# A recurrent attention layer with a SwiGLU layer behind it: the first feed-forward group in two halves of 256 columns, under a new emission order

## The chip, the cores and the metric

The kernel runs on one core of one Trainium2 chip. The metric is the device time of one execution in microseconds (us), lower is better. One execution was also recorded by the hardware profiler; its record (the trace) lists every instruction with start, duration and what it waited for. Names of engines: PE is the matrix engine, DVE the vector engine, ACT the scalar engine, POOL the fourth compute engine, SP the engine whose queue issues most transfers.

## The reference, cut to what matters

Inputs r, k, v, w have the shape (batch 4, head 8, time 768, 48), u is (8, 48). Per batch and head a 48x48 state is decayed by w and fed by k and v; its read-out by r, over all heads, is one row of 384 numbers per batch and time. These 3072 rows go through a normalised SwiGLU layer with 1536 inner columns.

```
for t in range(S):
    cur = einsum('bhd,bhe->bhde', u[None] * kt, vt)
    y[:, :, t] = einsum('bhd,bhde->bhe', rt, state + cur)
    state = wt[:, :, :, None] * state + einsum('bhd,bhe->bhde', kt, vt)
...
rms = sqrt(mean(x * x, axis=-1) + 1e-06)
xn = x / rms * rms_g
g = xn @ w_gate
out = (g * sigmoid(g) * (xn @ w_val)) @ w_out
```

## The kernel before, in words

Time is cut into six chunks of 128 steps. A chunk n of a batch j is a unit (n, j); there are 24 of them. A unit is handled in matrix form by small functions, each called a step and written as fn.n.j:

- load_r, load_k, load_v, load_w bring 192 KB each through the queue of SP (L259, L271). For chunks 0 and 1 one load_w of 384 KB (L271, form 128x8x96) serves both chunks of a batch. load_gv and load_wo bring the three weight matrices through the queue of POOL (L351, L354); load_gv.0.0 and 0.1 are the first 512 columns of w_gate and w_val, load_gv.1.0 and 1.1 the other 1024.
- ln (ACT), cs_mm (PE, L404 to L422), exp_r and exp_k (ACT), w_tot, r_mul and k_mul make the decayed r and k. k_mul runs on POOL or DVE, by a set of units called K_POOL (L459).
- rk_pe and rk_tr (L482, L489, L491) or a transposing transfer (L487) turn r and k; q_mm (L500, L502) gives the scores, q_mask_e and q_mask_o mask them (DVE L507, L515, or ACT L511 and POOL L518), y_mm (L545, L548) sums, st_mm and st_new carry the state. bonus_mul, bonus_sum, bonus_v are the u term (POOL, DVE, POOL).
- x_add, x_sq, x_rstd, xn_mul, then xn_pe and xn_out (L586, L596) or xn_tr and xn_gain, write the normalised, turned rows of the unit into its columns of a tile xnt.

The feed-forward layer works on groups of 512 columns, four units each. COL gives a unit its group and place: group 0 holds (0,0), (0,1), (1,0), (1,1) in this order, group 1 holds (0,2), (1,2), (0,3), (1,3), and groups 2 to 5 are the chunks 2 to 5. A group has 12 gate_mm and 12 val_mm steps. Each fills one PSUM bank of 512 columns with three matmuls of 512 columns for one of the 12 blocks of inner columns (L617). For a group named in HALF it fills the bank with two blocks of 256 columns, six matmuls in all (L622): steps f = 0 to 5 read only the first 256 columns of the group, f = 6 to 11 only the last 256. silu (ACT, L251) and h_mul (DVE, L643 or L646) take the banks away. o_mm (L660) multiplies with w_out, o_out copies, out_dma stores.

No scheduler orders this. The table ORDER at the head of the file lists all steps; the code runs through it once, and every engine executes its own steps in that order. A number behind a colon, as in `q_mm.1.1:7`, puts that many matmuls on a tile of zeros in front of the step (L238, L240); their result is overwritten. PSUM banks come from three rings (two slots for gate and cs_mm, two for val and cs_mm, four for the rest), and sets such as CAST_ACT, K_POOL, RK_DVE, ODD_DVE, RSTD_ACT and OUT_DVE say which engine does a step of a unit.

```
HALF = (1,)
...
def half_of_group(f):
    h, p = f // (FC // 2), f % (FC // 2)
    return slice(h * TS // 2, (h + 1) * TS // 2), 2 * p
...
for fn, n, j in steps:
    fns[fn](n, j)
```

Of the kernel before, what the change touches and what calls it, by code (L numbers as in the profile page):

```python
# [26 lines left out]
load_k.0.1 load_w.0.3 load_v.0.1 exp_r.0.0 exp_k.0.0 r_mul.0.0 cast_v.0.0 load_r.0.1 bonus_mul.0.0 load_k.1.1
bonus_sum.0.0 bonus_v.0.0 k_mul.0.0 cs_mm.1.0 load_r.1.1 load_v.1.1 load_v.1.0 load_w.0.2 rk_pe.0.0:2 rk_tr.0.0
exp_r.1.0 w_tot.1.0 w_tot.0.0 st_mm.0.0 r_mul.1.0 st_new.0.0 q_mm.0.0:4 load_k.0.3 load_r.0.3 load_r.0.2 load_k.0.2
load_v.0.2 ln.0.1 q_mask_o.0.0 exp_k.1.0 cs_mm.0.1 exp_r.0.1 k_mul.1.0 exp_k.0.1 rk_pe.1.0 load_v.0.3 rk_tr.1.0  # L30
bonus_mul.1.0 q_mask_e.0.0 load_k.1.3 load_r.1.2 load_k.1.2 load_r.1.3 load_v.1.2 bonus_mul.0.1 load_w.2.1 load_w.2.0
load_v.1.3 load_w.2.3 q_mm.1.0:2 cs_mm.1.1 exp_r.1.1 exp_k.1.1 r_mul.0.1 k_mul.0.1 w_tot.0.1 q_mask_o.1.0
bonus_sum.1.0 load_gv.0.1 cast_v.0.1 load_r.2.0 bonus_sum.0.1 r_mul.1.1 load_w.2.2 rk_pe.0.1:2 ln.0.3 y_mm.0.0
rk_tr.0.1 st_mm.0.1:4 x_add.0.0 q_mask_e.1.0 st_new.0.1 cs_mm.0.3:3 bonus_v.0.1 cast_v.1.0 q_mm.0.1:1 y_mm.1.0
k_mul.1.1 bonus_v.1.0 cast_v.1.1 q_copy_o.0.1 x_sq.0.0 bonus_mul.1.1 load_r.2.1 x_add.1.0 exp_r.0.3 load_r.2.2
x_sq.1.0 load_r.2.3 load_k.2.0 q_mask_e.0.1 w_tot.1.1 rk_pe.1.1:1 rk_tr.1.1 q_mm.1.1:7 q_mask_o.1.1 load_gv.0.0
q_mask_o.0.1 y_mm.0.1:8 g_mm.0.0 bonus_sum.1.1 ln.0.2 x_rstd.1.0 xn_mul.1.0 x_rstd.0.0 xn_mul.0.0 exp_k.0.3
bonus_v.1.1 load_gv.1.0 q_mask_e.1.1 x_add.0.1 x_sq.0.1 x_rstd.0.1 y_mm.1.1 x_add.1.1 k_mul.0.3 xn_pe.1.0:2 xn_pe.0.0
cs_mm.0.2 g_out.0.0 xn_out.1.0 x_sq.1.1 xn_mul.0.1 xn_out.0.0 r_mul.0.3 st_mm.1.1:3 x_rstd.1.1 st_mm.1.0 xn_mul.1.1
xn_pe.0.1 xn_out.0.1 w_tot.0.3 rk_pe.0.3:3 xn_pe.1.1 xn_out.1.1 exp_r.0.2 exp_k.0.2 r_mul.0.2 val_mm.0.0:4 gate_mm.0.3  # L40
silu.0.3 val_mm.0.3 rk_tr.0.3 w_tot.0.2 st_new.1.1 load_gv.1.1 k_mul.0.2 bonus_mul.0.2 q_mm.0.3 h_mul.0.3 st_new.1.0
gate_mm.0.2 gate_mm.0.0 rk_pe.0.2 silu.0.0 silu.0.2 val_mm.0.2 q_mask_e.0.3 h_mul.0.0 gate_mm.0.5 gate_mm.0.1 silu.0.5
silu.0.1 val_mm.0.1 rk_tr.0.2 q_copy_o.0.3 h_mul.0.1 bonus_mul.0.3 bonus_sum.0.3 h_mul.0.2 gate_mm.0.6:1
gate_mm.0.11:1 q_mm.0.2 cast_v.0.2 silu.0.6 silu.0.11 q_mask_o.0.2 gate_mm.0.8 val_mm.0.6 q_mask_e.0.2 cast_v.0.3
st_mm.0.2 val_mm.0.11 q_mask_o.0.3 h_mul.0.6 val_mm.0.5 y_mm.0.3 y_mm.0.2 bonus_sum.0.2 bonus_v.0.2 load_wo.0.0
load_wo.1.0 bonus_v.0.3 silu.0.8 h_mul.0.11 cs_mm.1.2 load_wo.2.0 h_mul.0.5 exp_k.1.2 x_add.0.2 st_new.0.2 exp_r.1.2
k_mul.1.2 cs_mm.1.3 exp_k.1.3 st_mm.0.3 exp_r.1.3 val_mm.0.8 val_mm.0.7 w_tot.1.2 r_mul.1.2 x_add.0.3 gate_mm.0.4
w_tot.1.3 r_mul.1.3 rk_pe.1.2 gate_mm.0.7 k_mul.1.3 h_mul.0.8 silu.0.4 x_sq.0.3 bonus_mul.1.2 x_rstd.0.3 rk_tr.1.2
silu.0.7 rk_pe.1.3 gate_mm.0.10 val_mm.0.4 h_mul.0.7 x_sq.0.2 rk_tr.1.3 load_k.2.1 load_k.2.3 load_v.2.1 load_v.2.0
load_k.2.2 q_mm.1.2 val_mm.0.9 cast_v.1.2 xn_mul.0.3 silu.0.10 q_copy_o.1.2 h_mul.0.4 q_mask_o.1.2 gate_mm.0.9  # L50
xn_pe.0.3 val_mm.0.10 st_new.0.3 q_mm.1.3 bonus_sum.1.2 x_rstd.0.2 q_mask_e.1.2 xn_out.0.3 y_mm.1.2 h_mul.0.10
q_mask_e.1.3 silu.0.9 h_mul.0.9 o_mm.0.3 ln.2.1 xn_mul.0.2 bonus_v.1.2 bonus_mul.1.3 q_mask_o.1.3 st_mm.1.2 xn_pe.0.2
cs_mm.2.1 ln.2.0 x_add.1.2 cs_add.2.1 x_sq.1.2 cs_mm.2.0 exp_r.2.1 o_out.0.3 xn_out.0.2 x_rstd.1.2 cast_v.1.3
cs_add.2.0 bonus_sum.1.3 w_tot.2.1 ln.2.3 exp_k.2.1 exp_r.2.0 o_mm.0.0 y_mm.1.3 xn_mul.1.2 o_out.0.0 bonus_v.1.3
r_mul.2.0 x_add.1.3 exp_k.2.0 ln.2.2 x_sq.1.3 o_mm.0.2 o_out.0.2 w_tot.2.0 r_mul.2.1 x_rstd.1.3 st_mm.1.3 cs_mm.2.3
xn_pe.1.2 cs_add.2.3 xn_out.1.2 cs_mm.2.2 exp_r.2.3 cs_add.2.2 load_k.3.3 w_tot.2.3 o_mm.0.1 xn_mul.1.3 r_mul.2.3
st_new.1.2 exp_k.2.2 val_mm.1.1 gate_mm.1.1 exp_r.2.2 exp_k.2.3 w_tot.2.2 val_mm.1.2 xn_pe.1.3 r_mul.2.2 gate_mm.1.2
st_new.1.3 silu.1.1 silu.1.2 k_mul.2.0 bonus_mul.2.0 out_dma.0.0 k_mul.2.1 cast_v.2.1 k_mul.2.3 h_mul.1.1 rk_tr.2.0
rk_tr.2.1 gate_mm.1.3 silu.1.3 bonus_mul.2.2 k_mul.2.2 xn_out.1.3 bonus_sum.2.0 h_mul.1.2 val_mm.1.5 gate_mm.1.4
silu.1.4 val_mm.1.4 rk_tr.2.3 gate_mm.1.8 st_mm.2.1 gate_mm.1.5 silu.1.8 h_mul.1.4 val_mm.1.8 load_v.2.2 silu.1.5  # L60
cast_v.2.0 st_new.2.1 rk_tr.2.2 o_out.0.1 h_mul.1.8 gate_mm.1.9 gate_mm.1.10 val_mm.1.3 load_w.3.3 load_v.2.3
load_r.3.3 load_w.3.1 out_dma.0.3 load_w.3.0 out_dma.0.1 load_r.3.0 bonus_v.2.0 bonus_mul.2.3 bonus_sum.2.2 h_mul.1.5
bonus_mul.2.1 cast_v.2.2 load_k.3.0 load_w.3.2 q_mm.2.0 load_k.3.1 silu.1.9 silu.1.10 q_copy_o.2.1 h_mul.1.3
q_mask_o.2.0 q_mask_e.2.0 q_mask_e.2.1 gate_mm.1.7 gate_mm.1.0 silu.1.0 val_mm.1.0 y_mm.2.0 gate_mm.1.6 val_mm.1.9
bonus_sum.2.3 h_mul.1.0 x_add.2.0 load_r.3.1 x_sq.2.0 silu.1.6 out_dma.0.2 h_mul.1.9 val_mm.1.10 h_mul.1.10 q_mm.2.2
gate_mm.1.11 val_mm.1.6 cast_v.2.3 q_copy_o.2.2 silu.1.7 silu.1.11 ln.3.0 x_rstd.2.0 xn_mul.2.0 q_mask_e.2.3
bonus_sum.2.1 q_mask_e.2.2 q_mask_o.2.1 load_v.3.3 load_w.4.1 load_r.3.2 ln.3.1 bonus_v.2.1 bonus_v.2.2 q_mask_o.2.3
h_mul.1.6 q_mask_o.2.2 bonus_v.2.3 st_mm.2.0 st_new.2.0 o_mm.1.0 y_mm.2.1 load_k.3.2 x_add.2.1 y_mm.2.3 val_mm.1.7
y_mm.2.2 cs_mm.3.0 st_mm.2.3 val_mm.1.11 x_add.2.3 x_sq.2.3 ln.3.3 x_sq.2.1 xn_pe.2.0 cs_mm.3.1 o_out.1.0 o_mm.1.1
out_dma.1.0 h_mul.1.7 cs_add.3.0 exp_k.3.0 x_add.2.2 cs_add.3.1 st_new.2.3 x_rstd.2.3 xn_mul.2.3 ln.3.2 x_sq.2.2  # L70
exp_r.3.0 x_rstd.2.1 k_mul.3.0 x_rstd.2.2 xn_out.2.0 exp_k.3.1 exp_r.3.1 xn_mul.2.1 xn_mul.2.2 h_mul.1.11 o_mm.1.2
r_mul.3.1 w_tot.3.0 k_mul.3.1 w_tot.3.1 xn_pe.2.1 bonus_mul.3.3 r_mul.3.0 o_out.1.2 xn_out.2.1 o_out.1.1 ln.4.1
cs_mm.3.3 xn_pe.2.2 cs_add.3.3 exp_r.3.3 rk_tr.3.1 rk_tr.3.0 cs_mm.3.2 cs_add.3.2 xn_pe.2.3 o_mm.1.3 bonus_mul.3.1
exp_r.3.2 xn_out.2.3 exp_k.3.2 w_tot.3.3 xn_out.2.2 w_tot.3.2 val_mm.2.2 st_mm.2.2 k_mul.3.2 exp_k.3.3 bonus_mul.3.0
r_mul.3.3 r_mul.3.2 gate_mm.2.8 gate_mm.2.2 val_mm.2.10 load_v.3.1 silu.2.8 silu.2.2 o_out.1.3 k_mul.3.3 st_new.2.2
h_mul.2.2 load_v.3.0 load_r.4.1 rk_tr.3.2 gate_mm.2.10 q_mm.3.0 cast_v.3.3 silu.2.10 q_copy_o.3.0 q_mask_e.3.1
bonus_sum.3.0 bonus_v.3.0 q_mask_o.3.0 cast_v.3.0 load_v.4.3 rk_tr.3.3 load_r.4.0 out_dma.1.2 gate_mm.2.9 val_mm.2.11
gate_mm.2.11 silu.2.9 h_mul.2.10 q_mask_e.3.0 val_mm.2.9 gate_mm.2.4 q_copy_o.3.1 bonus_sum.3.3 silu.2.11 bonus_v.3.3
h_mul.2.11 y_mm.3.0 val_mm.2.4 gate_mm.2.7 x_add.3.0 q_mm.3.2 h_mul.2.9 bonus_mul.3.2 silu.2.4 h_mul.2.4 load_v.3.2
gate_mm.2.3 cast_v.3.2 val_mm.2.3 val_mm.2.8 silu.2.3 q_copy_o.3.2 x_sq.3.0 q_copy_o.3.3 silu.2.7 load_k.4.0  # L80
load_k.4.1 load_w.4.0 x_rstd.3.0 xn_mul.3.0 q_mask_e.3.2 bonus_sum.3.1 gate_mm.2.5 h_mul.2.3 bonus_sum.3.2 h_mul.2.8
load_r.4.2 st_mm.3.3 val_mm.2.7 q_mask_e.3.3 st_mm.3.2 gate_mm.2.1 val_mm.2.1 silu.2.5 silu.2.1 q_mask_o.3.2
bonus_v.3.2 gate_mm.2.6 gate_mm.2.0 xn_pe.3.0 y_mm.3.2 st_new.3.2 load_w.5.0 cast_v.3.1 h_mul.2.1 h_mul.2.7 st_new.3.3
bonus_v.3.1 q_mask_o.3.1 out_dma.1.3 y_mm.3.1 val_mm.2.0 load_w.4.2 x_add.3.2 q_mask_o.3.3 silu.2.0 silu.2.6 h_mul.2.0
# [629 lines left out]
```

## Time and profile before

| what | value |
|---|---|
| time, median of 3 runs | 204.41 us (203.04, 204.41, 204.47) |
| span of the profiled execution | 202.2 us, 4604 instructions |
| median time less that span | 2.2 us |
| busy PE, DVE, ACT, POOL | 191.3, 157.5, 135.0, 124.4 us |
| moved by DMA | 32.42 MB, mean 160 GB/s |

The profiled execution's own time is not listed beside its span; the 2.2 us between its span and the median is what lies around a span here. Busy time is the union of an engine's instructions. A row of the timeline gives start, length, engine, line, operation, tiles, shapes and count, and in brackets the idle time before it and what ended it. A row of a windows view gives, for one stretch, busy time and number of instructions of each engine.

### The profile page before, as it was taken

Reading aid. Unit: us, or ns where it says so; the run is one execution under the profiler, and the core shown is the slowest. Engines: PE = TensorE matmul, PEld = TensorE weight load, DVE = VectorE, ACT = ScalarE, POOL = GpSimd, SP = SyncE. Lnnn points to the kernel's source line nnn. Section 1 sums busy time; section 2 is a strip of 40 time slices with the busy share of each in tenths; the row PEclk is TensorE's granted clock in tenths of the full one; section 3 lists DMA queues with packets and bytes.
Section 4 is the critical chain, followed back from the end, with each engine's and each line's share of the span. In section 5 each row is a group of like instructions: output and inputs, shape, how many; then the busy total and the mean of one; then the engine's idle time right before and its main releaser. Section 6 shows DMA issues by size and latency. Waiting matters only on the chain.

```text
span 202.2 us, 4604 instructions
## 1 busy us (share of the span) xinstructions
PE 191.3 (95%) x1677; PEld 121.9 (60%) x1694; DVE 157.5 (78%) x307; ACT 135.0 (67%) x278; POOL 124.4 (62%) x178
## 2 busy tenths in 40 slices
...
GB/s 144 231 234 207 212 208 202 195 179 208 206 184 225 160 212 191 210 185 188 199 176 215 237 188 203 183 190 108 134 179 104 0 23 99 0 117 0 63 115 99
DMA packets 121567, 32.42 MB, mean 160 GB/s; under 512 B 116420, under 2 KB 120392, under 8 KB 121544
## 3 DMA queue, kind: packets, MB, share of 16 engines
...
q10 hardware_dynamic: 8, 0.00, 0.0%
...
## 4 chain that ended last, share of the span: by engine, by line
PE 65%; ACT 3%; DMA 2%; DVE 2%; issue 1%; SPq 0%; DVEq 0%; ACTq 0%
PE ps_av L617 7%; PE ps_bu L617 7%; PE ps_au L617 7%; PE ps_bv L617 6%; PE ps_qx L660 6%; PE ps_qv L660 6%; PE ps_qu L660 5%; PE ps_qz L660 4%; PE ps_au L622 2%; PE ps_bu L622 2%; DMA rkT<-rk 2%; PE ps_av L622 2%; PE ps_bv L622 2%; ACT L249 1%; PE ps_au L419 1%; PE ps_qv L500 1%
## 5 line engine op out<-in xcount | busy, mean ns | idle before, releaser
L660 PEld LDWEIGHTS <-ht 128*128 128x128 bf16 x300 | 28.1, 98 | 17.5 <-DVE ht L646 1.0
L251 ACT ACTIVATE sg<-ps_av 128x512 bf16<-128x512 f32 x36 | 21.5, 597 | 22.8 <-PE ps_av L617 18.0
L646 DVE TENSOR_TENSOR ht<-ps_bv,sg 128x512 bf16<-128x512 f32 x29 | 19.9, 687 | 13.9 <-PE ps_bv L617 12.9
L251 ACT ACTIVATE sg<-ps_au 128x512 bf16<-128x512 f32 x36 | 21.5, 596 | 11.5 <-PE ps_au L617 7.7
L617 PEld LDWEIGHTS <-wg_sb 128*128 128x128 bf16 x180 | 19.2, 114 | 15.9 <-issue 0.6
L617 PEld LDWEIGHTS <-wv_sb 128*128 128x128 bf16 x180 | 19.2, 114 | 15.7 <-issue 0.5
L465 POOL TENSOR_TENSOR ruk<-rt,kt 128x384 f32<-128x384 f32 x24 | 24.0, 1001 | 3.7 <-DMA kt<-in_k_dram 2.8
L475 POOL TENSOR_TENSOR ydiag<-vt,diag 128x384 f32<-128x384 f32 x24 | 20.4, 859 | 9.4 <-DVE diag L470 9.1
L617 PE MATMUL ps_av<-xnt,wg_sb 128*128 128x512 bf16 x88 | 25.0, 381 | 0.3
L466 POOL TENSOR_TENSOR ruk<-ruk,u_bc 128x384 f32<-128x384 f32 x24 | 24.0, 1001 | 1.9
L617 PE MATMUL ps_bu<-xnt,wv_sb 128*128 128x512 bf16 x86 | 24.8, 380 | 0.4
L646 DVE TENSOR_TENSOR ht<-ps_bu,sg 128x512 bf16<-128x512 f32 x31 | 21.3, 686 | 4.8 <-PE ps_bu L617 3.1
L617 PE MATMUL ps_au<-xnt,wg_sb 128*128 128x512 bf16 x87 | 23.6, 380 | 0.1
L617 PE MATMUL ps_bv<-xnt,wv_sb 128*128 128x512 bf16 x82 | 23.2, 380 | 0.2
L459 POOL TENSOR_TENSOR rk<-kt,ek 128x384 bf16<-128x384 f32 x16 | 15.9, 1001 | 9.7 <-ACT ek L251 5.9
L249 ACT ACT_TABLE_LOAD x14 | 18.0, 1283 | 1.9 <-PEq L698 1.6
L660 PE MATMUL ps_qx<-wo_sb,ht 128*128 128x384 bf16 x96 | 17.1, 326 | 0.2 <-DVE ht L646 0.2
L558 ACT ACTIVATE junk<-xb 128x384 bf16<-128x384 f32 x24 | 12.5, 522 | 6.3 <-DVE xb L553 6.2
L571 ACT ACTIVATE xn<-xb,rstd 128x384 bf16<-128x384 f32 x24 | 14.2, 609 | 0.6 <-POOL rstd L567 0.5
L470 DVE TENSOR_REDUCE diag<-ruk 128x8 f32<-128x384 f32 x24 | 13.1, 544 | 1.9 <-POOL ruk L466 1.9
L660 PE MATMUL ps_qv<-wo_sb,ht 128*128 128x384 bf16 (+1 forms) x84 | 13.8, 314 | 0.0
L251 ACT ACTIVATE lw<-wt 128x384 bf16<-128x384 f32 (+1 forms) x20 | 11.6, 583 | 2.8 <-DMA wt<-in_w_dram 2.7
...
## 6 DMA issues: line engine op xcount, KB each, us to landing
...
wg_sb<-in_moe_w_gate_dram POOLq DMA_DIRECT2D x1, 768.0 KB, 9.2
```

What stands on the lines that cost most here:

```text
L249: nc.scalar.preload_act_table_set(table_name)
L251: return nc.scalar.activation(**kw).ins
L459: eng.tensor_tensor(out=rk[:, n % 2, j, 1, :, 0:D], in0=inp["k", n, j], in1=bank["cs_k", n, j][:, 0:DM].rearrange("p (h d) -> p h d", h=H) ...
L465: nc.gpsimd.tensor_tensor(out=ruk[n, j], in0=inp["r", n, j], in1=inp["k", n, j], op=ALU.mult)
L466: nc.gpsimd.tensor_tensor(out=ruk[n, j], in0=ruk[n, j], in1=u_bc, op=ALU.mult)
L470: nc.vector.tensor_reduce(out=diag[n, j].rearrange("p h o -> p (h o)"), in_=ruk[n, j], axis=mybir.AxisListType.X, op=ALU.add)
L475: nc.gpsimd.tensor_tensor(out=ydiag[n, j], in0=inp["v", n, j], in1=diag[n, j].to_broadcast([128, H, D]), op=ALU.mult)
L571: nc.scalar.activation(out=xn, in_=xb[n, j], func=AF.Copy, scale=rstd[n, j][:, 1:2])
L617: nc.tensor.matmul(ps, lhsT=units(ws, c, f), rhs=x[:, c, :], start=(c == 0), stop=(c == KC - 1))
L622: nc.tensor.matmul(ps[:, i * TS // 2:(i + 1) * TS // 2], lhsT=units(ws, c, f + i), rhs=x[:, c, cols], start=(i == 0 and c == 0), stop=(i = ...
L646: nc.vector.tensor_tensor(out=ht[n][:, f, :], in0=v, in1=sg, op=ALU.mult)
L660: nc.tensor.matmul(ps[:, cols], lhsT=ht[n][:, f, b * L:(b + 1) * L], rhs=wo_sb[:, f, cols], start=(f == 0), stop=(f == FC - 1))
```

## The change

HALF becomes (0, 1): group 0 too is computed in halves, the first from chunk 0 of batches 0 and 1, the second from chunk 1 of the same batches. The whole table ORDER is another one, without any number behind a colon, and eight sets are drawn anew. Functions and buffer counts stay as they are; every line number is one lower than before. The lines of the two sets Q_PAIR and OLD_DVE gain only a comma.

```
 ORDER = """
-load_r.0.0 load_w.0.0 u_mm.0.0 ln.0.0 load_v.0.0 load_k.0.0 cs_mm.0.0:2 load_r.1.0 load_w.0.1 u_out.0.0 load_k.1.0
...
+load_w.0.0 load_r.0.0 load_w.0.2 load_k.1.0 ln.0.0 load_v.0.0 cast_v.0.0 load_r.1.0 g_mm.0.0 u_mm.0.0 cs_mm.1.0
...
-    CAST_ACT = sel("00 01 02 03 20 21 30 31 33 40 43 53")
+    CAST_ACT = sel("01 10 12 20 21 23 30 33 50 51 53")
-    K_POOL = sel("02 10 20 21 22 23 30 31 32 33 40 42 43 50 51 53")
+    K_POOL = sel("02 03 12 13 21 22 23 30 31 32 40 41 43 50 52 53")
-    RK_DVE = sel("00 02 03 10 11 12 13")
-    ODD_DVE = sel("00 02 10 11 13 20 23 40 43 52")
-    RSTD_ACT = sel("00 10 11 13 20 32 33")
-    OUT_DVE = sel("00 01 10 13 20 21 22 30 33 40 42 50 52 53")
+    RK_DVE = sel("00 02 03 12 13")
+    ODD_DVE = sel("00 01 02 10 11 13 20 22 32 33 42 43 50")
+    RSTD_ACT = sel("00 01 10 11 23 33 42")
+    OUT_DVE = sel("00 02 11 13 21 22 30 31 32 41 43 51 53")
...
-    HALF = (1,)
+    HALF = (0, 1,)
```

Three places show what the new table does to the engines' own order. First the queue of SP at the start of the program, before; rt, kt, vt and wt are the tiles for r, k, v and w, and the units are, from the top, r(0,0), w of batch 0, v(0,0), k(0,0), r(1,0), w of batch 1, k(1,0) and k(0,1), w of batch 3, v(0,1).

```order
L259 DMA rt<-in_r_dram 128x8x48
L271 DMA wt<-in_w_dram 128x8x96
L259 DMA vt<-in_v_dram 128x8x48
L259 DMA kt<-in_k_dram 128x8x48
L259 DMA rt<-in_r_dram 128x8x48
L271 DMA wt<-in_w_dram 128x8x96
L259 DMA kt<-in_k_dram 128x8x48 x2
L271 DMA wt<-in_w_dram 128x8x96
L259 DMA vt<-in_v_dram 128x8x48
```

The same queue after: w of batch 0, r(0,0), w of batch 2, k(1,0), v(0,0), r(1,0), w of batch 1, k(0,0) and k(0,1).

```order
L270 DMA wt<-in_w_dram 128x8x96
L258 DMA rt<-in_r_dram 128x8x48
L270 DMA wt<-in_w_dram 128x8x96
L258 DMA kt<-in_k_dram 128x8x48
L258 DMA vt<-in_v_dram 128x8x48
L258 DMA rt<-in_r_dram 128x8x48
L270 DMA wt<-in_w_dram 128x8x96
L258 DMA kt<-in_k_dram 128x8x48 x2
```

Counted in loads of 192 KB, k(0,0) moved from the 5th to the 11th place, and v(0,1), a few rows further down, from the 13th to the 22nd. The second place is POOL's order from the first issue of a feed-forward weight to the last, before; ruk is bonus_mul's tile, ydiag bonus_v's, vb the cast v, rstd the scale of x_rstd.

```order
L351 DMA wv_sb_128<-in_moe_w_val_dram 128x3x512
L475 TENSOR_TENSOR ydiag<-vt,diag 128x384
L389 CAST vb<-vt 128x384
L475 TENSOR_TENSOR ydiag<-vt,diag 128x384
L389 CAST vb<-vt 128x384
L465 TENSOR_TENSOR ruk<-rt,kt 128x384
L466 TENSOR_TENSOR ruk<-ruk,u_bc 128x384
L351 DMA wg_sb_126<-in_moe_w_gate_dram 128x3x512
L518 AFFINE_SELECT qts<-qts 128x512
L475 TENSOR_TENSOR ydiag<-vt,diag 128x384
L351 DMA wg_sb_127<-in_moe_w_gate_dram 128x3x1024
```

After, over the same stretch and a little further:

```order
L350 DMA wv_sb_128<-in_moe_w_val_dram 128x3x512
L474 TENSOR_TENSOR ydiag<-vt,diag 128x384
L350 DMA wg_sb_126<-in_moe_w_gate_dram 128x3x512
L474 TENSOR_TENSOR ydiag<-vt,diag 128x384 x2
L388 CAST vb<-vt 128x384
L350 DMA wg_sb_127<-in_moe_w_gate_dram 128x3x1024
L458 TENSOR_TENSOR rk<-kt,ek 128x8x48
L464 TENSOR_TENSOR ruk<-rt,kt 128x384
L465 TENSOR_TENSOR ruk<-ruk,u_bc 128x384
L350 DMA wv_sb_129<-in_moe_w_val_dram 128x3x1024
```

The first three issues stand closer together now, and the last, w_val's other 1024 columns, stands behind k_mul and bonus_mul of unit (0,3); before, only two short operations of x_rstd (L566, L567) stood between the third and the last. The third place is DVE, from the last sum of group 0's units to the tile that the feed-forward matmuls read (xb is x_add's tile, xnt the group's), before:

```order
L507 TENSOR_TENSOR qts<-ps_qz,mask_lt 128x512
L553 TENSOR_TENSOR xb<-ps_qv,ydiag 128x384
L553 TENSOR_TENSOR xb<-ps_qx,ydiag 128x384
L459 TENSOR_TENSOR rk<-kt,ek 128x8x48
L382 COPY gT<-ps_qu 128x3
L596 TENSOR_TENSOR xnt<-ps_qz,gT 128x3x128
L596 TENSOR_TENSOR xnt<-ps_qv,gT 128x3x128
```

After:

```order
L552 TENSOR_TENSOR xb<-ps_qv,ydiag 128x384
L506 TENSOR_TENSOR qts<-ps_qz,mask_lt 128x512
L534 TENSOR_TENSOR st<-ps_qu,wcol 128x384
L514 TENSOR_TENSOR qts<-ps_qx,mask_lt 128x512
L552 TENSOR_TENSOR xb<-ps_qu,ydiag 128x384
L595 TENSOR_TENSOR xnt<-ps_qv,gT 128x3x128
L595 TENSOR_TENSOR xnt<-ps_qx,gT 128x3x128
```

Both masks of unit (1,1) and a state update now stand between the sums of (0,1) and (1,1), and the two xnt writes behind them are those of (0,0) and (0,1), all that the first half of group 0 reads; the writes of (1,0) and (1,1) come later. On PE two gate steps and one val step of the first half stand ahead of the first step of the second half; the xn_pe of (1,0) and (1,1) stand between them.

More of the change, by code (lines that the diff above doesn't have):

```diff
@@ L25 @@
 ORDER = """
-load_r.0.0 load_w.0.0 u_mm.0.0 ln.0.0 load_v.0.0 load_k.0.0 cs_mm.0.0:2 load_r.1.0 load_w.0.1 u_out.0.0 load_k.1.0
[L27 to L84, printed above, removed]
-ln.4.0 cast_v.4.3 val_mm.2.6 h_mul.2.6 y_mm.3.3 cs_mm.4.1 load_r.4.3 load_k.4.3 val_mm.2.5 cs_mm.4.0 x_add.3.1
@@ new lines @@
+xn_pe.0.0 st_mm.1.1 y_mm.1.1 x_sq.0.1 x_sq.1.0 x_rstd.0.1 exp_k.0.3 k_mul.0.3 x_add.1.1 xn_out.0.0 x_rstd.1.0
+xn_mul.0.1 xn_mul.1.0 bonus_mul.0.3 load_gv.1.1 xn_pe.0.1 xn_out.0.1 w_tot.0.2 r_mul.0.2 x_sq.1.1 k_mul.0.2 rk_pe.0.3
+x_rstd.1.1 gate_mm.0.0 xn_pe.1.0 gate_mm.0.1 xn_mul.1.1 st_new.1.1 st_mm.1.0 rk_tr.0.3 xn_out.1.0 load_k.1.2 xn_pe.1.1
+val_mm.0.1 xn_out.1.1 silu.0.0 silu.0.1 q_mm.0.3 gate_mm.0.7 load_w.2.1 val_mm.0.0 gate_mm.0.6 st_new.1.0 h_mul.0.1
+q_mask_e.0.3 h_mul.0.0 silu.0.7 silu.0.6 load_v.1.2 val_mm.0.6 gate_mm.0.8 val_mm.0.7 gate_mm.0.9 bonus_mul.0.2
```

137 lines of the change are left out of this document (95 added, 42 removed).

## The prediction

> **What bounds the kernel now.** I read the page's busy times first, then PE by stretches, then what PE waits for behind the start.
>
> ```profile
> span 202.2 us, 4604 instructions
> PE 191.3 (95%) x1677; PEld 121.9 (60%) x1694; DVE 157.5 (78%) x307; ACT 135.0 (67%) x278; POOL 124.4 (62%) x178
> ```
>
> PE is busy for 95% of the span. The windows view, cut at the first feed-forward matmul (30.21 us) and at PE's end (199.03), says where the rest lies. PE is the first number behind the length of the stretch.
>
> ```profile
> core 0: us, PE busy (x) PEld busy (x) DVE busy (x) ACT busy (x) POOL busy (x), PEclk, DMA share, GB/s
> 0.00:30.21 30.21, 24.25 (x284) 16.16 (x285) 22.14 (x51) 18.06 (x40) 21.78 (x38) 1.00 1.03 206
> 30.21:199.03 168.82, 167.02 (x1394) 105.72 (x1409) 135.04 (x256) 116.91 (x239) 102.63 (x141) 1.00 0.73 153
> 199.03:202.20 3.17, 0.00 (x0) 0.00 (x0) 0.36 (x1) 0.00 (x0) 0.00 (x0) 0.86 0.27 96
> ```
>
> In the middle PE idles 168.82 - 167.02 = 1.8 us. So the time is a start of 30.2 us, a stretch in which PE is the bound, and an end of 3.2 us. Whatever comes off PE's work there comes off the time, and each new wait of PE is added to it. Moving loads and vector work about changes nothing by itself. Of PE's waits from 29 us on the view of waits names two:
>
> ```profile
> PE ps_qu L500 <- DMA rkT<-rk: 0.6, 1, 0.6
> PE ps_qx L660 <- DVE ht L646: 0.2, 1, 0.2
> ```
>
> The start differs in kind: PE's 24.25 us there hold many matmuls on zeros. The L240 group by stretches (the L238 group adds 30 matmuls, all before 30 us):
>
> ```profile
> 12.00:30.00 18.00, 6.30 (x32) 2.85 (x32) 1.00 1.13 211
> 36.00:39.00 3.00, 0.65 (x2) 0.20 (x2) 1.00 1.16 218
> ```
>
> **Part 1: the halves themselves.** A step of group 1, already in halves, and one of group 2 in the chain of work:
>
> ```profile
> 66.53 0.66 PE ps_bv L622 x6
> 92.85 0.65 PE ps_au L617 x3
> ```
>
> Six matmuls of 256 columns take as long as three of 512, within 0.01 us (0.655 against 0.648 by the steps' distances). 24 steps cost 24 x 0.007 = **+0.17 us**. silu and h_mul read banks of the same 512 columns, so ACT and DVE pay nothing. No work is saved: the halves only permit the first half to start before chunk 1 is ready. As the order rows in the sections above show, the table uses that for three steps only.
>
> **Part 2: the zero matmuls go.** Those before 30 us stand in front of steps that wait, so their time is a wait otherwise, and its cover is the chain that the start hangs on (part 3). The two at 36 to 39 us stand between real matmuls:
>
> ```profile
> 36.94 0.33 PE L240 MATMUL ps_av<-zero 128*128 128x384 bf16 x1
> 37.10 0.81 PE L617 MATMUL ps_av<-xnt,wg_sb 128*128 128x512 bf16 x3
> 37.74 0.33 PE L240 MATMUL ps_au<-zero 128*128 128x384 bf16 x1
> 37.91 0.81 PE L617 MATMUL ps_au<-xnt,wg_sb 128*128 128x512 bf16 x3
> ```
>
> From start to next start they take 0.16 and 0.17: **-0.33 us**, all on the path.
>
> **Part 3: the start, with late loads.** Two POOL rows give the pace of the loads: bonus_mul waits for k(0,0), fifth in units of 192 KB; the first cast waits for v(1,0), eighteenth.
>
> ```profile
> 7.08 1.00 POOL L465 TENSOR_TENSOR ruk<-rt,kt 128x384 f32<-128x384 f32 x1 [2.84 <-DMA kt<-in_k_dram]
> 19.11 0.50 POOL L389 CAST vb<-vt 128x384 bf16<-128x384 f32 x1 [0.62 <-DMA vt<-in_v_dram]
> ```
>
> (19.11 - 7.08) / 13 = 0.925 us a load, with the queue full. k(0,0), now eleventh, is there at 7.08 + 6 x 0.925 = 12.6 us. k_mul.0.0 follows, and rk_pe.0.0 starts at 13.1 instead of 9.98. v(0,1), now twenty-second, lands at 19.11 + 4 x 0.925 = 22.8; its cast takes 0.5, so y_mm.0.1 starts at 23.4 at the earliest and, behind DVE's masks, I estimate 24.7. It started at 24.28. The rows from there:
>
> ```profile
> 9.98 0.70 PE L482 MATMUL ps_qv<-ident,rk 128*128 128x128 bf16 x8
> 24.28 0.19 PE L548 MATMUL ps_qv<-vb,qts 128*128 128x48 bf16 x1
> 25.92 0.56 DVE L553 TENSOR_TENSOR xb<-ps_qx,ydiag 128x384 f32<-128x384 f32 x1 [0.30 <-PE ps_qx L548]
> 29.40 0.81 PE L240 MATMUL ps_bv<-zero 128*128 128x384 bf16 x4
> 30.21 0.81 PE L617 MATMUL ps_bv<-xnt,wv_sb 128*128 128x512 bf16 x2
> 32.58 0.84 PE L617 MATMUL ps_au<-xnt,wg_sb 128*128 128x512 bf16 x3
> 16.03 0.36 PE L548 MATMUL ps_qz<-vb,qts 128*128 128x48 bf16 x8
> 18.72 0.55 DVE L535 TENSOR_TENSOR st<-ps_qu,wcol 128x384 bf16<-128x384 f32 x1
> 24.14 0.68 DVE L507 TENSOR_TENSOR qts<-ps_qz,mask_lt 128x512 bf16<-128x512 f32 x1
> 29.93 1.28 ACT L249 ACT_TABLE_LOAD   x1
> ```
>
> Behind y_mm.0.1 DVE has x_add (0.56), a mask (0.68), st_new (0.55), a mask (0.68), then x_add.1.1 (0.56) behind its y_mm (0.36): about 3.4 us, so x_add.1.1 ends near 28.2 instead of 26.48. The xnt writes of (0,0) and (0,1) end a microsecond later, at some 29.6, and the first gate starts there, 0.6 ahead of 30.21. Its bank is free again only after silu, which stands behind xn_mul.1.1 and the table load of 1.28: about 32.8. So the fourth feed-forward step starts at 32.8, where it started at 32.58 before. With the matrix engine at full pace the early half gains nothing: the bounds of this term are -0.6 (the head start is kept) and +0.2.
>
> What the zeros covered is PE's own pace. The same two matmuls of cs_mm, cold and later:
>
> ```profile
> 6.35 0.85 PE L404 MATMUL ps_au<-lw,mw 128*128 128x384 bf16 x2
> 6.99 0.40 PE L408 MATMUL ps_au<-mw,lw 128*128 128x1 bf16 x8
> 11.80 0.50 PE L404 MATMUL ps_au<-lw,mw 128*128 128x384 bf16 x2
> 12.13 0.34 PE L408 MATMUL ps_au<-mw,lw 128*128 128x1 bf16 x8
> ```
>
> From L404 to L408 it is 0.64 us first and 0.33 later: half pace until PE had worked through some 6 us without a pause. (The windows' granted clock says 1.00 all along; it is the distances that show it.) In the changed kernel it waits from about 9 to 13 us, and between 24 and 29.6 its real work is y_mm, st_mm, q_mm, xn_pe and rk_pe: an estimated 2.1 us of 5.6 by their counts and the distances of such rows. If that lets the pace drop, three feed-forward steps (1.95 us), xn_pe, st_mm and q_mm (0.8) run at half pace: +2.7 less the 0.6 of head start, and up to 1 us more where PE is the chain before. I take **+1.9 us**; bounds -0.6 and +3.7. I lean to the slow side since the nearest row is the cold one, in which PE had just been idle.
>
> The Trainium skill, page "TensorE: Matmul & The Clock Gate", Part 1, says that the clock is halved by default, is released after about 3.4 us of sustained work, and is halved again after an idle window of as much. The trace agrees on the factor of two and shows about 6 us instead of 3.4 here. By that rule a wait such as 9 to 13 us could close the gate, but the thinner work from 13 to 29 would leave it open, and this term would be about 0; that outcome is the first rival.
>
> **Part 4: the weights.** The last three issues on POOL's queue, and k_mul of a unit of chunk 0 there:
>
> ```profile
> 23.15 0.81 POOL L351 DMA_DIRECT2D wg_sb<-in_moe_w_gate_dram  x1
> 25.35 0.80 POOL L351 DMA_DIRECT2D wg_sb<-in_moe_w_gate_dram  x1
> 27.36 0.85 POOL L351 DMA_DIRECT2D wv_sb<-in_moe_w_val_dram  x1
> 30.00 0.99 POOL L459 TENSOR_TENSOR rk<-kt,ek 128x384 bf16<-128x384 f32 x1 [1.78 <-ACT ek L251]
> ```
>
> From the view of DMA issues, the KB and the us from issue to landing of the two large parts:
>
> ```profile
> wg_sb<-in_moe_w_gate_dram POOLq DMA_DIRECT2D x1, 768.0 KB, 9.2
> wv_sb<-in_moe_w_val_dram POOLq DMA_DIRECT2D x1, 768.0 KB, 11.5
> ```
>
> The last w_val part was issued at 27.36 and landed at 27.36 + 11.5 = 38.9, the w_gate part before it at 25.35 + 9.2 = 34.5; its first reader came at 39.66. Now it stands behind k_mul.0.3 and bonus_mul.0.3, three operations of 1.0, the first of which waits for exp_k.0.3: some 30.7, so it lands between 39.3 (4.4 behind a w_gate part that itself lands some 0.4 later than now) and 30.7 + 11.5 = 42.2. Its first reader, val_mm.0.8, is the 13th step: 32.8 + 9 x 0.655 + 0.45 = 39.2, or 41 at half pace. The wait is 0 to 3; with the slow start most of it is covered. I take **+0.3**.
>
> **Part 5: the rest of the order.** Sums of work on every engine hardly move: DVE gains three masks of 0.68 and loses two rkT copies and one o_out. PE idles 1.8 us in the middle now. It can lose all of that (-1.8): between the last cs_mm and q_mm.4.0 stand six feed-forward steps behind o_mm.2.2 where four stood, which would take up the wait of 0.6 for rkT. It can also gain. Between q_mm.3.2 and the first y_mm that needs it stand three steps (2.0 us), where nine stood, while DVE has four masks of 0.68 to do in that time. One such place costs up to 0.7, and there are eight pairs of units. Bounds -1.8 and +5; I take **+0.8**, one such place, nearer to the trace's own 1.8 than to the far end.
>
> The end is the same: a half o_mm, a copy and a store, 3.17 us. From the last y_mm to the first gate of group 5 four o_mm of 1.95 each and two steps stand, where three o_mm and seven steps stood, 9.1 us against 10.4; a row of the chain for one o_mm:
>
> ```profile
> 87.00 1.95 PE ps_qv L660 x12
> ```
>
> **The sum:** 202.2 + 0.17 - 0.33 + 1.9 + 0.3 + 0.8 = 205.0 us of span. The median stands 2.2 above the profiled span; kept, that gives 207.2 us, 1.4% over 204.41. One per cent, 2.0 us, is about what a measurement of this kernel can tell from no change.
>
> **Rivals.**
> *The pace holds.* PE works thinly but never pauses for long after 13 us, so nothing runs at half pace. Then the start costs +0.2, the weights +0.7 since nothing covers them: 202.2 + 0.17 - 0.33 + 0.2 + 0.7 + 0.8 = 203.7, time 205.9. For it: from 13 us there is always some PE work. Against it: no row shows PE at full pace on thin work.
> *Not slower.* The head start is kept, because silu's table load comes early enough, and the longer distance to q_mm.4.0 and q_mm.5.0 takes up two thirds of PE's idle: 202.2 + 0.17 - 0.33 - 0.6 - 1.2 = 200.2, time 202.4. It decides if the fourth feed-forward step starts before 32.2. Against it: v(0,1) at 22.8.
> *Crowded masks.* DVE, 135 of 168.82 us busy in the middle, cannot follow at the shortened places, and at all eight pairs PE waits some 0.6: +5 instead of +0.8, time 211.4. For it: DVE's share; against it: the masks and the steps there take nearly the same time by the rows.
>
> **Chances.** Forecast 0.42, pace holds 0.27, not slower 0.11, crowded masks 0.20. The first lies above 206.4 in four cases of five, the last always, the second hardly ever: slower 0.56. Faster needs the third rival and more: 0.09. Within 1%: 0.35. The range 202.9 to 211.4 leaves out the faster half of the third rival and the far half of the last. The likeliest case alone spans 205.0 to 209.
>
> **What would show it.** Part 1: L621 groups of six 0.655 us apart. Part 2: no L239. Part 3: k(0,0)'s multiplication at 12.6, the first L621 matmul at 29.6 and its next steps 1.3 us long instead of 0.65; if they take 0.65, the pace held. Part 4: a PE wait before a val step near 40 us. Part 5: PE idle between 40 us and the last matmul, 1.8 now, 2.6 by this forecast, above 5 for the last rival. The prediction is wrong if the fourth feed-forward step starts before 32 us or PE's idle in the middle falls below 1.

## The result, and the profile after

The changed kernel takes 207.14 us (median of four runs, 206.46 to 207.5), the kernel before 204.22 us (median of four, 203.04 to 204.47): a ratio of 1.0151, 95% interval 1.012 to 1.0182. A ratio leaves out executions over 1.5% above the fastest of their kernel, at most one in each run below, but five of twelve in a_loads_z and in a_best. The profiled execution took 206.84 us, its span is 205.1 us, against 202.2 before. So the time came out where it was forecast, but not by the forecast's reasons.

First the top of the page of the changed kernel, with the lines that answer to those of before:

```profile
span 205.1 us, 4622 instructions
PE 186.7 (91%) x1696; PEld 124.9 (61%) x1696; DVE 157.9 (77%) x307; ACT 136.0 (66%) x277; POOL 123.1 (60%) x176
```

PE does 4.6 us less (the zero matmuls are gone), and the span is 2.9 us longer. The windows view of the changed kernel, cut again at the first feed-forward matmul and at PE's end:

```profile
0.00:28.23 28.23, 17.70 (x207) 10.83 (x208) 20.47 (x49) 18.34 (x40) 19.68 (x34) 1.00 1.04 208
28.23:201.66 173.43, 168.95 (x1490) 114.05 (x1489) 137.39 (x260) 117.39 (x238) 103.40 (x143) 1.00 0.72 151
201.66:205.10 3.44, 0.00 (x0) 0.00 (x0) 0.00 (x0) 0.32 (x1) 0.00 (x0) 1.00 0.33 117
```

The start ended earlier, at 28.23 instead of 30.21. In the middle PE idles 173.43 - 168.95 = 4.5 us where it idled 1.8. Since the two cuts don't stand at the same amount of work, I compare from the start of the fourth feed-forward step on. In the timeline of the changed kernel:

```profile
11.44 0.55 DVE L458 TENSOR_TENSOR rk<-kt,ps_bv 128x384 bf16<-128x384 f32 x1 [0.36 <-DMA kt<-in_k_dram]
28.23 0.81 PE L621 MATMUL ps_au<-xnt,wg_sb 128*128 128x256 bf16 x6 [0.20 <-DVE xnt L595]
29.42 1.28 ACT L248 ACT_TABLE_LOAD   x1
31.36 0.84 PE L621 MATMUL ps_au<-xnt,wg_sb 128*128 128x256 bf16 x6
38.44 0.85 PE L621 MATMUL ps_bv<-xnt,wv_sb 128*128 128x256 bf16 x6 [0.55 <-DVE diag L469]
```

The fourth step starts at 31.36 instead of 32.58: the start gained 1.22 us. From there to PE's end it is 201.66 - 31.36 = 170.30 us, where it was 199.03 - 32.58 = 166.45: the rest lost 3.85. The end is 0.27 longer (3.44 against 3.17). Together: -1.22 + 3.85 + 0.27 = 2.9 us.

Where the rest lost it, the view of PE's waits from 28.3 us on begins to say:

```profile
PE ps_qx L499 <- DMA rkT<-rk: 1.5, 1, 1.5
PE ps_qu L499 <- DMA rkT<-rk: 1.0, 1, 1.0
PE ps_bv L621 <- DVE diag L469: 0.5, 1, 0.5
PE ps_av L418 <- ACT lw L250: 0.5, 1, 0.5
PE ps_qv L499 <- DVE ht L645: 0.4, 1, 0.4
PE ps_av L616 <- POOL xnt L601: 0.3, 1, 0.3
```

Two q_mm steps wait for a turned rk: q_mm.2.0 at 72 us and q_mm.5.0 at 155 us. The wait at 38.44 us stands with a DVE step that had long been done; in the view of the weight loads it reads `PEld L621 <- DMA wv_sb<-in_moe_w_val_dram: 0.8, 1, 0.8`, the late part of w_val. That is an account of places, not yet of a cause. The chain that ended last, followed back, is one; its pieces around 64 to 92 us in the changed kernel (start, length, what):

```profile
63.85 0.39 SPq L486
64.25 0.06 issue
64.30 4.13 DMA kt<-in_k_dram
68.47 0.09 issue
68.57 1.00 POOL rk L458
69.57 0.96 POOL ruk L464
...
85.33 4.59 DMA kt<-in_k_dram
89.96 0.09 issue
90.05 1.96 POOL rk L458 x2
```

The work there hangs on loads of k. The load of k(2,3) is issued at 64.30 since SP was held by the turning transfer ahead of it; between these pieces the chain runs through one issue of SP after the other, from 74.7 to 85.3 us. How much the transfers brought in that time is the last number of the windows view (GB/s, behind the share of the 16 DMA engines). 60 to 70 us before, and then after:

```profile
60.00:70.00 10.00, 10.00 (x100) 8.96 (x99) 8.15 (x18) 7.94 (x17) 9.61 (x11) 1.00 1.11 188
```

```profile
60.00:70.00 10.00, 10.00 (x100) 9.42 (x99) 9.32 (x21) 8.09 (x16) 6.49 (x8) 1.00 0.67 114
```

74 GB/s less over 10 us are 0.74 MB, nearly four loads of 192 KB. In the other windows of 10 us from 10 to 130 us the share is 0.84 or more in both kernels, so the lag is made up only slowly: from 80 to 100 us the changed kernel moves 211 and 205 GB/s, the kernel before 181 and 189. The load of k at 85.33 is again one that POOL waits for.

### The profile page after: what moved, and what is told of

Read it like the earlier page. It is cut to its first block, busy times and chain, and to the rows that moved or that the text cites. A ratio compares the mean times of both kernels' runs of the same rounds, so it can differ in the third digit from the quotient of the medians.

```text
span 205.1 us, 4622 instructions
## 1 busy us (share of the span) xinstructions
PE 186.7 (91%) x1696; PEld 124.9 (61%) x1696; DVE 157.9 (77%) x307; ACT 136.0 (66%) x277; POOL 123.1 (60%) x176
## 4 chain that ended last, share of the span: by engine, by line
PE 36%; DMA 17%; ACT 13%; POOL 13%; SPq 8%; DVE 6%; issue 5%; POOLq 0%; DVEq 0%; ACTq 0%
DMA kt<-in_k_dram 6%; PE ps_av L616 6%; PE ps_bv L616 5%; PE ps_au L616 4%; DMA xnt<-xn 4%; PE ps_bu L616 4%; SPq L258 4%; POOL rk L458 4%; PE ps_qx L659 3%; SPq L270 3%; DMA wo_sb<-in_moe_w_out_dram 3%; POOL ruk L464 3%; ACT xn L570 3%; POOL ruk L465 3%; DMA rkT<-rk 2%
## 5 line engine op out<-in xcount | busy, mean ns | idle before, releaser
L616 PEld LDWEIGHTS <-wg_sb 128*128 128x128 bf16 x144 | 15.7, 114 | 13.9 <-issue 0.8
L645 DVE TENSOR_TENSOR ht<-ps_bv,sg 128x512 bf16<-128x512 f32 x25 | 17.1, 685 | 8.7 <-PE ps_bv L616 8.4
L616 PEld LDWEIGHTS <-wv_sb 128*128 128x128 bf16 x144 | 15.5, 114 | 12.5
L616 PE MATMUL ps_av<-xnt,wg_sb 128*128 128x512 bf16 x75 | 20.3, 379 | 0.3 <-POOL xnt L601 0.3
L616 PE MATMUL ps_bv<-xnt,wv_sb 128*128 128x512 bf16 x75 | 20.4, 380 | 0.0
L645 DVE TENSOR_TENSOR ht<-ps_bu,sg 128x512 bf16<-128x512 f32 x23 | 15.8, 687 | 4.4 <-PE ps_bu L616 3.7
L616 PE MATMUL ps_au<-xnt,wg_sb 128*128 128x512 bf16 x69 | 18.7, 380 | 0.0
L616 PE MATMUL ps_bu<-xnt,wv_sb 128*128 128x512 bf16 x69 | 18.7, 380 | 0.0
L659 PE MATMUL ps_qx<-wo_sb,ht 128*128 128x384 bf16 (+1 forms) x96 | 15.9, 316 | 0.0
L621 PEld LDWEIGHTS <-wv_sb 128*128 128x128 bf16 x144 | 15.1, 114 | 1.3 <-DMA wv_sb<-in_moe_w_val_dram 0.8
L621 PEld LDWEIGHTS <-wg_sb 128*128 128x128 bf16 x144 | 15.1, 114 | 0.8 <-issue 0.3
L659 PE MATMUL ps_qu<-wo_sb,ht 128*128 128x384 bf16 x84 | 14.8, 326 | 0.0
```

What stands on the lines that cost most here:

```text
L616: nc.tensor.matmul(ps, lhsT=units(ws, c, f), rhs=x[:, c, :], start=(c == 0), stop=(c == KC - 1))
L621: nc.tensor.matmul(ps[:, i * TS // 2:(i + 1) * TS // 2], lhsT=units(ws, c, f + i), rhs=x[:, c, cols], start=(i == 0 and c == 0), stop=(i = ...
L645: nc.vector.tensor_tensor(out=ht[n][:, f, :], in0=v, in1=sg, op=ALU.mult)
L659: nc.tensor.matmul(ps[:, cols], lhsT=ht[n][:, f, b * L:(b + 1) * L], rhs=wo_sb[:, f, cols], start=(f == 0), stop=(f == FC - 1))
```

## The experiments

Each was timed beside the kernel before on the same chip. The theory I began with: the start gained, and a few new waits, each with a cause of its own, cost the rest. Against it stood general crowding, in which a wait that is removed comes back next door, and the forecast's own theory of PE's pace. The theory that held, late loads, was formed after the first four runs.

**b_half.** The kernel before with group 0 in halves, in its own order; blocks renamed so that the first weights are still used first.

```diff
-    HALF = (1,)
+    HALF = (0, 1)
-... val_mm.0.0:4 gate_mm.0.3 silu.0.3 val_mm.0.3 ...
+... val_mm.0.0:4 gate_mm.0.7 silu.0.7 val_mm.0.7 ...
```

> The kernel before with group 0 in halves and nothing else: same table, zeros kept, only the twelve blocks renamed (2 to 6, 3 to 7, 4 to 2, 5 to 3, 6 to 4, 7 to 5) so that the first four steps still read the weights that come first. Theory 'halves are free' (the prediction's part 1): 24 steps 0.007 us longer, +0.2 us, 204.4 us. Rival 'halves cost': twice as many loads of weights into PE, not all hidden, +1 us or more, 205.2 or above.

205.51 us, ratio 1.008 (1.0043 to 1.0116): +0.9 to +2.4 us, nearer to the rival, but not for the rival's reason. The steps are about 0.66 us apart, as forecast. The profile shows other waits: 0.7 at the first o_mm for the last product (0.2 before), and at 175 us

```profile
175.44 0.81 PE L617 MATMUL ps_av<-xnt,wg_sb 128*128 128x512 bf16 x3 [1.10 <-POOL xnt L602]
```

a wait for a turning transfer that landed later than in the kernel before, though nothing near it in the order had changed. Whether these waits belong to the halves is not settled by one profile.

**b_nozero.** The kernel before without zero matmuls.

```diff
-load_r.0.0 load_w.0.0 u_mm.0.0 ln.0.0 load_v.0.0 load_k.0.0 cs_mm.0.0:2 ...
+load_r.0.0 load_w.0.0 u_mm.0.0 ln.0.0 load_v.0.0 load_k.0.0 cs_mm.0.0 ...
```

> The kernel before without one number behind a colon, so without its zero matmuls; the output is complete. Theory 'the pace holds on thin work': the two zeros at 36 to 39 us are saved and nothing else moves, -0.3 us, 203.9 us. Rival, the prediction's part 3: the start and the first feed-forward steps run at half pace, +2 us or more, 206 us or above, with steps 1.3 us apart at 30 us.

204.62 us, ratio 1.0044 (1.0015 to 1.0073): between the two. The pace did fall. The windows view of b_nozero, where the third number from the end is the granted clock:

```profile
24.00:28.00 4.00, 3.47 (x42) 2.83 (x43) 3.30 (x7) 3.69 (x12) 3.07 (x5) 0.59 1.05 174
28.00:32.00 4.00, 3.35 (x35) 2.73 (x34) 3.02 (x7) 3.43 (x9) 2.17 (x3) 0.56 1.21 232
```

The first feed-forward step comes at 31.70 instead of 30.21, but from there on the steps are 0.65 apart, and part of the 1.5 us is won back behind: the wait of 0.6 for rkT that the kernel before had is gone.

**a_sp2.** The changed kernel; SP's queue freed ahead of one turning transfer.

```diff
 rk_tr.2.0
-load_v.2.0
...
-out_dma.0.1
...
 rk_tr.2.1
+load_v.2.0 out_dma.0.1
```

> The changed kernel with one edit: on SP's queue the load of v(2,0) and a store of group 0 go behind the transfer that turns r and k of unit (2,1). Theory 'few waits, each of its own': the wait of 1.5 us of the scores step of (2,0) goes, 205.8 us (-1.3). Rival 'general crowding': another wait takes its place within the same stage, 206.8 us or above.

207.31 us, ratio 1.0164 (1.013 to 1.0199): no gain. The wait of q_mm.2.0 is gone, and two others stand at 90 and 76 us, the rows of 1.2 and 0.5 in the view of PE's waits of a_sp2 (that of 1.0 is q_mm.5.0 as before):

```profile
PE ps_qu L584 <- ACT ob L667: 1.2, 1, 1.2
PE ps_qu L498 <- DMA rkT<-rk: 1.0, 1, 1.0
PE ps_qx L498 <- DMA rkT<-rk: 0.5, 1, 0.5
```

**a_fix3.** The same edit, and two more at the waits of 119 and 155 us.

```diff
-o_out.2.3
...
 ln.4.3
+o_out.2.3
...
 exp_r.5.0
+exp_k.5.0
...
+k_mul.5.0
 bonus_mul.5.2
...
+rk_tr.5.0
 out_dma.3.1
```

> The changed kernel with the edit of a_sp2 and two more: on ACT the copy of an output of group 2 goes behind the logarithm of (4,3); and for unit (5,0) the exponential, the multiplication and the turning transfer go ahead of the ACT, POOL and SP work that stood in front of them. Theory 'few waits': waits of 1.5, 0.5 and 1.0 us go, of the last at least half, 204.6 us (-2.3 to -2.9). Rival 'general crowding': under 1 us gained, 206.2 or above.

206.95 us, ratio 1.0117 (1.0056 to 1.0178), with times near 205.7 and near 208.5 and none between. That is 0.7 us by the ratios, inside their intervals, of 2.3 to 2.9 expected. In the profiled execution (208.06 us) PE waits 1.38 for the copy of an output near 90 us, as in a_sp2, and 0.95 for xn_gain.4.3, which k_mul.5.0 had pushed back on POOL. So "a few waits, each of its own" falls. What the waits of 70 to 100 us have in common is the chain shown above, and that gave the theory of the next run.

**a_loads.** The changed kernel; four loads go ahead of the turning transfer for which SP stood still.

```diff
+load_k.2.3 load_v.2.0 load_v.2.2 load_v.2.3
 rk_tr.2.2
-load_k.2.3
...
 rk_tr.2.0
-load_v.2.0
...
-load_v.2.2 load_v.2.3
 load_v.3.1
```

> The changed kernel with four loads moved on SP's queue: k(2,3), v(2,0), v(2,2) and v(2,3) go ahead of the turning transfer of (2,2), which SP waits for from 58.3 to 62.9 us with nothing issued. Theory 'late loads': from 60 to 70 us the transfers move 114 GB/s where the kernel before moved 188, and what was not brought then makes every input late until 100 us; the share of DMA in that stretch goes back to about 1, the waits at 72 and 96 us go, 205.2 us (-2). Rival 'crowded queues of POOL, ACT and DVE': loads are not what is late, 206.8 or above.

203.82 us, ratio 0.999 (0.9954 to 1.0025): the whole loss is gone, 0.0161 in ratio or 3.3 us from four moved issues. The slowest of twelve executions, 205.29 us, lies below the fastest of the changed kernel, 206.46. SP's queue (timeline, one row for neighbours of a kind) in the changed kernel:

```profile
57.17 0.38 SPq L258 DMA_DIRECT2D vt<-in_v_dram  x1
57.60 0.74 SPq L258 DMA_DIRECT2D kt<-in_k_dram  x1
62.92 1.33 SPq L486 DMA_TRANSPOSE rkT<-rk  x1
64.30 0.57 SPq L258 DMA_DIRECT2D kt<-in_k_dram  x1
64.98 2.41 SPq L486 DMA_TRANSPOSE rkT<-rk  x1
```

and in a_loads:

```profile
57.10 0.39 SPq L257 DMA_DIRECT2D vt<-in_v_dram  x1
57.53 2.35 SPq L257 DMA_DIRECT2D kt<-in_k_dram  x2
59.98 2.41 SPq L257 DMA_DIRECT2D vt<-in_v_dram  x3
65.31 2.68 SPq L485 DMA_TRANSPOSE rkT<-rk  x2
```

From 58.3 to 62.9 us SP had waited for r and k of (2,2) with four loads behind it that waited for nothing. With them ahead, the 60 to 70 us window moves more, though less than the 188 GB/s of before (windows view of a_loads):

```profile
60.00:70.00 10.00, 10.00 (x107) 8.81 (x106) 8.43 (x19) 7.93 (x16) 8.15 (x10) 1.00 0.91 139
```

So the bytes of these 10 us do not decide it: a_zero below moves 138 GB/s in them and keeps its loss. What differs is when they move. From 60 to 64 us, with SP held, after, and then with the four loads ahead, a_loads:

```profile
60.00:64.00 4.00, 4.00 (x40) 3.47 (x39) 3.60 (x10) 3.74 (x8) 2.42 (x3) 1.00 0.22 45
```

```profile
60.00:64.00 4.00, 4.00 (x46) 2.85 (x45) 3.08 (x8) 2.52 (x6) 2.39 (x4) 1.00 1.13 222
```

The kernel before moves 209 there and a_zero 34. a_loads has a gap of its own from 64 to 68 us (93 GB/s) and pays nothing that can be measured for it. POOL's waits for loads of k, in the changed kernel:

```profile
68.57 1.00 POOL L458 TENSOR_TENSOR rk<-kt,ek 128x384 bf16<-128x384 f32 x1 [1.76 <-DMA kt<-in_k_dram]
90.05 1.96 POOL L458 TENSOR_TENSOR rk<-kt,ek 128x384 bf16<-128x384 f32 x2 [2.32 <-DMA kt<-in_k_dram]
```

are gone in a_loads, where the same steps wait for nothing or for ACT:

```profile
68.21 1.98 POOL L457 TENSOR_TENSOR rk<-kt,ek 128x384 bf16<-128x384 f32 x2
89.17 1.00 POOL L457 TENSOR_TENSOR rk<-kt,ek 128x384 bf16<-128x384 f32 x1 [0.66 <-ACT ek L249]
```

Its view of PE's waits from 30 us on has one row left:

```profile
PE ps_qu L498 <- DMA rkT<-rk: 0.4, 1, 0.4
```

The waits at 96, 119 and 178 us went too, without an edit near them. That they hung on the same loads is the likely reading, not shown for each. The one at 72 us is not shown to be the edit's work either: the profiled execution of a_loads began its feed-forward steps late (below) and reached q_mm.2.0 at 73.09 us, 2.41 behind the changed kernel's 70.68, while the turning transfer waited for there, that of (2,1), was issued at 69.99, later than the 68.75 of the changed kernel. So the times show that the four loads were the cause; which wait each of them made, this profile doesn't.

**b_late.** The kernel before with the opposite edit.

```diff
-load_v.2.0 load_k.2.2
...
-load_k.3.3
...
 rk_tr.2.0 rk_tr.2.1
+load_k.2.2 load_k.3.3 load_v.2.0
```

> The kernel before with the opposite edit: v(2,0), k(3,3) and k(2,2) go behind the turning transfers of (2,0) and (2,1) on SP's queue. Theory 'late loads': a gap of the transfers near 60 us as in the changed kernel and a wait for rkT near 75 us that wasn't there, +1 us or more, 205 us or above. Rival: three loads have room, 204.1 us, no change.

204.25 us, ratio 1.003 (0.9999 to 1.0061): the sign fits, the size is below what I expected and barely above nothing. The profiled execution, which took 206.44 us, moves 161 GB/s from 60 to 70 us, where 188 stood before and 114 in the changed kernel: the edit opened a smaller gap. That this is why it cost less is a guess.

**h_w22 and s_k12.** The two grafts.

```diff
 (table of the changed kernel up to) w_tot.2.2
+(every other step, in the order of the kernel before)
```

> A graft: the changed kernel's table up to w_tot.2.2 (the start, group 0 in halves and the units of chunk 1, to about 58 us), then every step that is left in the order of the kernel before, without its zeros, with the sets of each for its own units. Theory 'the start gains 1 us, the rest of the new table loses': 203.2 us, under both kernels. Rival 'the loss is in the start, its halves and its weights': 206 us or above.

206.82 us, ratio 1.0137 (1.0095 to 1.0179).

```diff
 (table before, with zeros, up to) k_mul.1.2
+(every other step, in the order of the changed kernel)
```

> The opposite graft: the table before up to k_mul.1.2 with its zeros (group 0 in halves with the same blocks first), then what is left in the order of the changed kernel. Theory 'the start gains, the rest loses': the slowest of all, 208 us (+1 over the changed kernel). Rival 'the loss is in the start': 204.5 us.

215.24 us, ratio 1.0541 (1.0492 to 1.059). Neither splits the loss between start and rest, since each seam opens waits that neither table has: s_k12 waits 4.3 us for silu at two places and moves 61 GB/s from 60 to 70 us; h_w22 moves 105 there. h_w22 lies nearer the rival, s_k12 beyond both. I leave them out of the argument.

**a_k23.** Of the four loads only k(2,3).

```diff
+load_k.2.3
 rk_tr.2.2
-load_k.2.3
```

> The changed kernel with one load moved, k(2,3) ahead of the turning transfer of (2,2); the three v loads stay. Theory 'one late input': POOL waited for k(2,3) until 68.57 us and both waits hang on it, so nearly all of the gain of a_loads comes, 204.2 us. Rival 'backlog of transfers': the bytes not moved from 58 to 70 us count, one load of four gives a quarter of the gain, 206.2 us.

206.01 us, ratio 1.0104 (1.0053 to 1.0155): some 30% of the gain of a_loads by the middle values, near the rival's quarter, though the interval runs from nothing to some 60%. k(2,3) alone was not it. Nor was it the place of the turning transfer of (2,2) itself: it is issued at 64.93 here and at 65.31 in a_loads, and only a_loads gets the whole back. POOL now waits for a v load:

```profile
74.90 1.62 POOL L473 TENSOR_TENSOR ydiag<-vt,diag 128x384 f32<-128x384 f32 x2 [1.03 <-DMA vt<-in_v_dram]
```

**a_zero.** The changed kernel with zeros in PE's early waits.

```diff
-... rk_pe.0.0 ... q_mm.1.0 ... rk_pe.0.1 ... rk_pe.1.1 ... y_mm.0.1 ... st_mm.1.1 ... xn_pe.0.0 ... y_mm.1.1 ... xn_pe.0.1
+... rk_pe.0.0:4 ... q_mm.1.0:4 ... rk_pe.0.1:2 ... rk_pe.1.1:2 ... y_mm.0.1:1 ... st_mm.1.1:2 ... xn_pe.0.0:2 ... y_mm.1.1:1 ... xn_pe.0.1:5
```

> The changed kernel with zero matmuls put into PE's waits from 9 to 28 us (numbers behind nine steps, 4 4 2 2 1 2 2 1 5), nothing else. Theory 'the pace falls in some executions': the full pace at 28 us comes every time, the times lie closer together, and the median falls by up to 0.7 us, 206.4 us. Rival 'the pace was held in the changed kernel anyway': no gain, 207.1 us or, since zeros delay real steps, a little more.

206.82 us, ratio 1.0156 (1.0119 to 1.0192): the same as the changed kernel. The clock is 1.00 in every window from 9 to 40 us and the fourth feed-forward step starts at 30.91, 0.45 earlier, yet nothing comes of it: PE waits 2.2 us for rkT in three places, 0.6 each for xnt and for w_val, and less for others. The likely reading is that while loads are late, an earlier start only means a longer wait for them. It is a weak test of the pace, since the profiled execution of the changed kernel had kept it from 20 us on as well.

**a_loads_z and a_best.** Both edits; then also the last weight part earlier.

```diff
+load_gv.1.1
 k_mul.0.3
...
-load_gv.1.1
```

> Both edits, the four loads of a_loads and the zeros of a_zero. Theory 'a_loads has two times, one with the pace held and one without': only its lower group is left, 202.4 us with little spread, under the kernel before. Rival 'its spread has another cause': 203.8 us as a_loads, with the same spread.

Median 205.0 us, ratio 1.0017 (0.9985 to 1.0049), times from 203.23 to 207.42: no gain over a_loads, and the spread grew. The zeros did not keep the pace in the profiled execution (granted clock 0.69 from 24 to 28 us), and its fourth feed-forward step came at 33.89, behind v(0,1), for which ACT waited until 24.44. So what the pace is worth once the loads are in time isn't settled by this run.

> a_loads_z with the last part of w_val issued on POOL ahead of the multiplication of k(0,3) instead of three operations later. Theory 'the late weights cost what PE waited at 38 us': another 0.6 us, 201.8 us. Rival 'the weights then take the transfers of the inputs': no gain, 202.4 us or above.

Median 204.44 us, ratio 0.9984 (0.9952 to 1.0016), times from 202.05 to 207.34. By the middle values that is 0.7 us, but the intervals overlap, and in the profiled execution of a_loads_z PE had no wait for w_val that could be saved. No version here beats the kernel before by an amount that can be measured.

## Why the prediction came out right, and which steps were wrong

*Parts 1 and 2.* Steps of six matmuls are 0.655 us apart, and no L239 is left. But "the halves only permit" was too light: in the old order they cost +0.9 to +2.4 us (b_half), though the profile doesn't settle through which wait.

*Part 3, the start (+1.9).* Wrong for the profiled execution, which gained 1.22: k(0,0) was multiplied at 11.44 and not 12.6, y(0,1) came at 23.12 and not 24.7, the table load ended at 30.7, and the pace, half up to some 15 us (L403 to L407 still 0.63 apart at 14.28), held from 20 us on. The signal that I named for a wrong prediction, a fourth step before 32 us, occurred. The mechanism, though, is real. Five more profiled executions share this start up to 57 us; their fourth step came at 31.72 (a_fix3), 32.03 (a_sp2), 34.31 (a_k23), 34.40 (a_loads) and 34.78 (h_w22), the last four at half pace for a while. a_loads, from 24 to 32 us:

```profile
24.00:28.00 4.00, 2.23 (x39) 1.55 (x39) 3.49 (x8) 3.90 (x14) 0.80 (x1) 0.88 1.21 211
28.00:32.00 4.00, 3.91 (x26) 3.23 (x27) 3.40 (x8) 3.88 (x9) 3.90 (x6) 0.50 1.15 211
```

The forecast's 32.8 with the pace held stands 1.4 and 1.1 us too late for the two that held it (31.36 and 31.72); 32.58 + 1.9, or 34.5, without it fits three of the four others. What I had not seen is that with late loads this term hardly enters the time: a_zero's earlier start gains nothing. What it is worth with the loads in time stays open.

*Part 4, the weights (+0.3, bounds 0 to 3).* PE's weight load waited 0.8 for the w_val part (PE itself idled 0.55), close to the 0.7 that the rival took for a held pace.

*Part 5, the rest of the order (+0.8, bounds -1.8 and +5).* Mis-sized, and the place was wrong. PE's idle in the middle, the sign named for it, was 4.5 and not 2.6. By the account above the rest, without the 0.8 for weights (0.55 would do as well) and with 0.17 - 0.33 for parts 1 and 2, lost 3.85 - 0.8 + 0.16 = 3.2 us; a_loads gives 3.3 in the total. That the two agree is partly chance, since the split is that of one execution: in the profiled one of a_loads the fourth step came at 34.40, 1.82 behind the kernel before, and PE's end some 165.3 us later, 1.2 less than before. I had looked for it at DVE's masks. The sentence that failed stands at the head of the prediction: "Moving loads and vector work about changes nothing by itself." It does here: four loads on SP's queue are worth 3.3 us. In the windows of before the share of the transfers is 0.84 or more from 10 to 130 us, which the prediction did not look at. How much of the cost comes from that crowding is not shown, and the bytes alone are not it: a_loads moves fewer than the kernel before from 60 to 70 us and loses nothing. The turning transfers stand in SP's queue with the loads, and the prediction counted the steps between them and their readers (q_mm.4.0), not the loads behind them.

*The sum.* +1.9 forecast against -1.2 at the start, and +0.8 against +3.2 behind it: an error of 3.1 us against errors of 2.4, 0.5 (weights) and 0.3 (the end) with the other sign, so that 207.2 against 207.14 is luck. The rival "pace holds" had the start nearer, and "crowded masks" the size of the rest, with a different cause.
